# Gated attention and a mixture of experts on one core: the first group's third and fourth expert multiply their first layers in parts

## The chip, the core and the metric

The kernel runs on one core of a Trainium2 chip. A core has five engines, each with its own instruction queue that is worked off in order: PE (TensorE, matmuls; its weight loads are listed as PEld), DVE (VectorE), ACT (ScalarE), POOL (GpSimd) and SP (SyncE, which here only issues DMAs). The engines wait for each other through semaphores. The metric is device time of one launch in microseconds (us); lower is better.

## The reference

Attention with a gated state gives x, and a dense mixture of four experts follows. Everything is float32.

```python
# q, k, v, alpha: (B, H, S, D) = (4, 8, 768, 48)
for t in range(S):
    state = alpha[:, :, t, :, None] * state + np.einsum('bhd,bhe->bhde', k[:, :, t], v[:, :, t])
    y[:, :, t] = np.einsum('bhd,bhde->bhe', q[:, :, t], state)
x = y.transpose(0, 2, 1, 3).reshape(B * S, H * D)          # (3072, 384)
p = domain_probs / (domain_probs.sum(-1, keepdims=True) + 1e-09)
for e in range(4):                                         # w1: (4, 384, 1024), w2: (4, 1024, 384)
    h = np.maximum(x @ w1[e], 0.0)
    out += p[:, e:e + 1] * (h @ w2[e])
```

## The kernel before

**Units and groups.** The attention is worked in 24 units, each 128 tokens of one batch entry (`attention(u)`, a generator that yields after each step). A unit ends in 128 columns of x, written to a tile `x_raw`. The experts take the units in groups: the first group (`gi == 0`) has two units, so 256 tokens; five groups of four units (512 tokens) follow, and a last one of two. For each group the four experts run one after the other, each as a first layer (`up`, eight tiles of 128 hidden rows) and a second layer (`down`, eight steps over the hidden rows for each unit). In the first group the experts are taken in the order 1, 2, 3, 0 (`real`); "the third expert" is the one at `e == 2`, "the fourth" that at `e == 3`.

**Products in parts.** From the second group on, a first-layer tile is not one float32 product. w1 is split into a rounded top and the rest (tile `w1`, two parts; `split_piece`: an ACT copy and a DVE subtraction for each quarter of an expert), x likewise into top and low (tile `xT`; `split_x`: three ACT copies, then three DVE subtractions by `split_rest`), and a rounded copy of w1 (tile `w1s`) is loaded by a casting DMA on POOL's queue (`load_short`). Nine matmuls in the reduced format fp32r give one tile: top by top, rest by top, and `w1s` by low, for each of three row blocks. The first group instead multiplies x and w1 as they are, with three full float32 matmuls per tile (L849), while its weights are split beside it and written to DRAM tiles `kept`, from which later groups load them.

**Buffers.** `w1` and `w1s` have four buffers each, one expert. The first group's raw w1 lies in `w2r` and `w2` buffers that nobody else uses yet (`shared`); that of the fourth expert lies in `w1s` buffers (`last_w1`). The first group's x lies in the second half of its `xT` tile; later groups have `x_raw`, with one buffer.

**Order.** The order of instructions is fixed when the program is built. `advance` moves a model clock by `cost(...)` after every tile of the experts, and takes the next steps of attention units when their due times (`deal`) have come; `background` starts splits (`making`, `splitting`) and casting loads (`casts`) at the end of each tile. So an attention step stands in each engine's queue between the experts' instructions, and its place follows from the model clock, not from the chip. `cost` gives 2.6 for a tile of the first group's first layer for a full width of four units, 2.1 for one in parts.

Names that the prediction uses, with the lines of the kernel before: `one` (PSUM of a first-layer tile: L849 in full, L855 in parts), relu into `hT` (L851), `ops` (second layer, L936), accumulate into `acc` (L958), splits (L282 on ACT, L284 on DVE, L275 a POOL cast of w2), `kept` writes (L290), `w1s` loads (L232), x splits (L806 ACT, L306 DVE). Of attention: transposes `tp` (L321), scores `sc` (L607, L683, L688), `odd` and `qb` (ACT copies of q), `KT` and `QT` products (L600, L586), `lat` (score copies, ACT L698 and L701, POOL L706), result `yps` (L728), AT copy of the keys (L752), state product `sps` (L768), state update `st` (L778, L779).

Of the kernel before, what the change touches and what calls it, by code (L numbers as in the profile page):

```python
# [20 lines left out]
def kernel(  # L21
# [137 lines left out]
    last_w1 = {}  # L159
# [74 lines left out]
    def load_piece(l, i, beside=False, rest=False):  # L234
        if i >= E * NQ * LAST:
            return
        gi, k = divmod(i, E * NQ)
        e, c = divmod(k, NQ)
        if gi > l and not (l == 1 and fresh(gi, e)):
            if l == 0:  # L240
                w, short = wt[l][i] = first_parts(), first_short()
                nc.sync.dma_start(out=w.bitcast(F32), in_=kept[l][k])
                casts.append((beat[0], lambda: load_short(l, i, short)))
                return
            w = second(rest)
            nc.sync.dma_start(out=w[:, :1].bitcast(F32), in_=kept[l][k][:, 1:] if rest else kept[l][k][:, :1])
            if not rest:
                casts.append((beat[0], lambda: load_short(l, i, w[:, 1])))
            wt[l].setdefault(i, []).append(w)
            return  # L250
        if l == 1 and gi == 0 and not beside:
            return
        if l == 0:

            if e == 0:
                shared[c] = second(True)[:, 0], second(False)[:, 1]
            if e == E - 1:
                last_w1[c] = first_short()
            w = (last_w1[c] if e == E - 1 else shared[c][e % 2]).bitcast(F32)
        elif gi > 0 or e == 1:  # L260
            if c == 0:
                shared["w2"] = hid.tile([P, NQ, KC * QF], F32, name="raw2", bufs=1)
            w = shared["w2"][:, c]
        else:
            w = hidden[c][:, 0].rearrange("p f n -> p (f n)")[:, :KC * QF].bitcast(F32)
        wt[l][i] = w
        nc.sync.dma_start(out=w.rearrange("p (c n) -> p c n", c=(KC, FPQ)[l]), in_=whole_piece(l, i))

    def split_piece(l, i):
        gi, k = divmod(i, E * NQ)  # L270
        whole = wt[l][i]
        if i >= E * NQ:
            ws = wt[l][i] = [second(False), second(True)]
            top, rest = (w[:, 0] for w in ws)
            nc.gpsimd.tensor_copy(out=ws[0][:, 1], in_=whole)  # L275
        else:
            ws = [first_parts()]
            top, rest = (ws[0][:, part] for part in range(2))
            if k // NQ == E - 1:
                last_w1[k % NQ] = ws[0]  # L280
# [22 lines left out]
    def split_rest(x, out):  # L303

        top, low = out
        nc.vector.tensor_sub(low, x, top.bitcast(F32))  # L306

# [16 lines left out]
    def first_unit(fill, other):  # L324
# [160 lines left out]
        xTs[0] = work.tile([P, 2, KC, NT], F32R, name="xT", bufs=1)  # L485
        xraws[0] = xTs[0][:, 1].bitcast(F32)
# [29 lines left out]
    def attention(u):  # L516
# [197 lines left out]
        def result():  # L714
# [16 lines left out]
            if slot == 0:  # L731
                if gi == 0:
                    xTs[gi] = work.tile([P, 2, KC, NT], F32R, name="xT", bufs=1)
                    xraws[gi] = xTs[gi][:, 1].bitcast(F32)
                elif gi < LAST:
                    xraws[gi] = work.tile([P, KC * NT + PAD], F32, name="x_raw", bufs=1)[:, :KC * NT]
                    xraws[gi] = xraws[gi].rearrange("p (c n) -> p c n", n=NT)
                else:
                    xraws[gi] = []
# [71 lines left out]
    def up(gi, e, fc, slots=None):  # L811
# [16 lines left out]
        if gi == 0 and e > 0 and fc in SPLIT_AT:  # L828
            making.append(split_piece(0, e * NQ + SPLIT_AT[fc]))
        if gi == 0 and e == E - 1 and fc in (3, 6):  # L830
            making.append(split_piece(1, E * NQ + 1 + fc // 3))
# [6 lines left out]
        if gi > 0:  # L838
# [8 lines left out]
        if gi == 0:  # L847
            for kc in range(KC):
                nc.tensor.matmul(one, lhsT=w[:, kc], rhs=xraws[gi][:, kc, lo:hi],  # L849
                                 start=(kc == 0), stop=(kc == KC - 1))  # L850
            nc.scalar.activation(out=whole, in_=one, func=ACT.Relu)  # L851
        else:
            for part in (1, 2, 0):
                for kc in range(KC):
                    nc.tensor.matmul(one, lhsT=short[:, kc] if part == 1 else w[:, part // 2, kc], rhs=x_part(gi, part % 2, kc)[:, lo:hi],  # L855
                                     start=(part == 1 and kc == 0), stop=(part == 0 and kc == KC - 1))
# [7 lines left out]
        if f == FPQ - 1 and ends:  # L864
            if gi == 0:
                for k in range(2 if e == E - 2 and c > 1 else 0):
                    load_piece(0, (E - 1) * NQ + 2 * (c - 2) + k)
# [3 lines left out]
                if e == E - 1:  # L871
                    wt[0][E * NQ + c] = last_w1[c], first_short()
                    casts.append((beat[0], lambda: load_short(0, E * NQ + c, wt[0][E * NQ + c][1])))
# [13 lines left out]
    def down(gi, e, slots, between):  # L887
# [4 lines left out]
        if gi == 0 and e < E - 1 and slots[0] == (e == 0):  # L892
            making.extend(split_piece(0, first + NQ + k) for k in range(2))
        if gi == 0 and e == E - 2 and slots[0] == 1:
            making.extend(split_piece(1, E * NQ + k) for k in range(NQ // 2))
# [76 lines left out]
    def cost(layer, gi, e):  # L972
        n = len(groups[gi]) / 4
        if layer == 0:
            return 1.4 * n if fresh(gi, e) else 2.1 * n if gi > 0 else 2.6 * n
# [60 lines left out]
    with tc.manual_schedule():  # L1036
# [42 lines left out]
        for (gi, e), after in zip(tasks, [*tasks[1:], (None, None)]):  # L1079
            pieces = portions(gi, e)  # L1080
            for part in pieces:
# [6 lines left out]
                for k, slots in enumerate(turns):  # L1088
                    between = deque()
                    if following:  # L1090
# [35 lines left out]
```

## Time and profile before

| | |
|---|---|
| median of 3 runs | 965.45 us (964.46 to 966.07) |
| the profiled execution | 963.51 us; span of its instructions 961.7 us |
| PE busy | 953.7 us (99%) |
| DVE, ACT, POOL busy | 535.1, 419.2, 246.6 us |
| granted TensorE clock | 1.00 throughout |
| DMA | 246.48 MB, mean 256 GB/s |
| first group's third expert | first layer from 77.17 us, second from 91.92 us |
| first group's fourth expert | first layer from 106.27 us, second from 120.65 us |

All views come from one profiled execution. Its span is the time from the first to the last instruction; the execution's own time lies 1.8 us above it. Busy time counts what an engine executes, not what it waits for; a row of the timeline gives start, duration, engine, line, operation and, in brackets, the idle time before it and what ended it. The duration of a matmul is longer than the step to the next one, since matmuls overlap; steps are read from start to start. A full float32 matmul appears as two rows' worth of records.

### The profile page before, as it was taken

How to read it: one execution, taken by the hardware profiler on the slowest of the kernel's cores; microseconds unless marked ns; L12 is line 12 of the kernel's file. 1: busy time of each engine (PE TensorE's matmuls, PEld its weight loads, DVE VectorE, ACT ScalarE, POOL GpSimd, SP SyncE). 2: the span in 40 equal slices, each digit the busy share in tenths (PEclk: the TensorE clock that was granted, in tenths of full speed). 3: DMA queues.
4: the chain of work that ended last, by engine and by line, in shares of the span. 5: the costliest groups of instructions: out<-in, count | busy, mean ns of one | idle time of the engine just before them, and what ended most of it. 6: DMA issues, size and time to landing. Idle time of an engine off the chain costs nothing.

```text
span 961.7 us, 24843 instructions
## 1 busy us (share of the span) xinstructions
PE 953.7 (99%) x10252; PEld 851.3 (89%) x10252; DVE 535.1 (56%) x1127; ACT 419.2 (44%) x975; POOL 246.6 (26%) x403
## 2 busy tenths in 40 slices
PE   8999999999999999999999999999999999999998
PEld 7777779898998988988989889899898899999998
DVE  6766887778588555655546456646764312221312
ACT  5786766536445434344344343555435222021111
POOL 3121423344245322313312222233221202020200
PEclk9999999999999999999999999999999999999999
DMA  9889867999799999999999799989997609192921
GB/s 223 264 279 318 244 177 230 275 310 311 206 359 322 305 309 318 236 339 303 273 311 270 259 316 296 342 247 270 305 309 264 230 1 354 41 324 70 303 91 50
DMA packets 213952, 246.48 MB, mean 256 GB/s; under 512 B 95152, under 2 KB 183600, under 8 KB 213840
## 3 DMA queue, kind: packets, MB, share of 16 engines
q1 hardware_dynamic: 158800, 160.02, 56.6%
q0 software_dynamic: 54592, 84.55, 30.8%
q8 instruction: 81, 1.33, 0.6%
q10 hardware_dynamic: 448, 0.32, 0.1%
q14 instruction: 31, 0.25, 0.1%
HBM read 214.97 MB, written 29.88 MB: 255 GB/s over the span
## 4 chain that ended last, share of the span: by engine, by line
PE 94%; DVE 2%; issue 1%; ACT 1%; DMA 1%; POOL 0%; SPq 0%; DVEq 0%; ACTq 0%; POOLq 0%
PE ops L936 41%; PE one L855 38%; PE yps L728 3%; PE one L849 3%; PE sc L607 3%; PE tp L321 2%; PE sc L683 1%; DMA sk<-in_k_dram 1%; PE sps L768 1%; PE sc L688 0%; DVE QT L586 0%; DVE w2r L284 0%; ACT qb L579 0%; PE sc L380 0%; DVE KT L600 0%
## 5 line engine op out<-in xcount | busy, mean ns | idle before, releaser
L936 PE MATMUL ops<-w,hT 128*128 128x384 f32 x1408 | 254.2, 338 | 0.0
L855 PE MATMUL one<-xT,w 128*128 128x512 f32 (+1 forms) x1008 | 246.7, 380 | 0.0
L936 PEld LDWEIGHTS ops<-w,hT 128*128 128x128 f32 x1408 | 243.3, 188 | 2.5 <-issue 0.2
L857 ACT ACTIVATE hT<-one 128x512 fp32r<-128x512 f32 (+1 forms) x200 | 108.6, 547 | 279.9 <-PE one L855 278.8
L884 DVE SCALAR_TENSOR_TENSOR hT<-one,hT 128x512 fp32r<-128x512 f32 (+1 forms) x200 | 124.7, 627 | 170.3 <-ACT hT L857 170.0
L855 PEld LDWEIGHTS one<-xT,w 128*128 128x128 f32 x1008 | 184.0, 188 | 36.7
L855 PE MATMUL one<-xT,w1s 128*128 128x512 f32 (+1 forms) x504 | 141.5, 389 | 0.0
L232 POOL DMA_DIRECT2D w1s<-in_moe_w_dram x80 | 62.5, 781 | 257.5 <-PE one L855 256.9
L936 PE MATMUL ops<-w2r,hT 128*128 128x384 f32 x704 | 127.8, 337 | 0.0
L936 PEld LDWEIGHTS ops<-w2r,hT 128*128 128x128 f32 x704 | 122.1, 188 | 0.3 <-issue 0.2
L579 ACT COPY qb<-QT 64x256 f32<-64x256 f32 x230 | 92.5, 402 | 33.0 <-DVE QT L586 31.2
L855 PEld LDWEIGHTS one<-xT,w1s 128*128 128x128 f32 x504 | 89.7, 188 | 16.0 <-DVE hT L884 0.4
L586 DVE TENSOR_TENSOR QT<-QT,AT 128x256 f32<-128x256 f32 x158 | 72.6, 460 | 32.6 <-ACT qb L579 24.4
L958 DVE SCALAR_TENSOR_TENSOR acc<-ops,p_all,acc 128x384 f32<-128x384 f32 x66 | 39.6, 612 | 86.1 <-PE ops L936 85.1
L600 DVE TENSOR_TENSOR KT<-KT,AT 128x256 f32<-128x256 f32 x161 | 75.8, 471 | 0.0
L617 DVE COPY_PREDICATED near<-masks,sc 128x128 f32<-128x128 uint8 x115 | 40.9, 355 | 61.8 <-PE sc L607 59.9
L706 POOL COPY lat<-near 32x256 f32<-32x256 f32 x92 | 45.6, 496 | 96.0 <-DVE near L617 92.7
L232 POOL DMA_DIRECT2D w<-in_moe_w_dram x60 | 43.4, 727 | 96.6 <-PE ops L936 76.6
L599 ACT COPY KT<-KT 128x256 f32<-128x256 f32 x115 | 47.2, 411 | 4.6 <-PE sc L607 2.4
L570 ACT ACTIVATE odd<-QT,ident 64x256 f32<-64x256 f32 x36 | 18.8, 523 | 69.7 <-DVE QT L528 69.4
L588 DVE TENSOR_TENSOR AT<-AT 128x256 f32<-128x256 f32 (+1 forms) x138 | 42.1, 305 | 4.7
L778 POOL TENSOR_TENSOR st<-st,dec 64x192 f32<-64x192 f32 x32 | 16.7, 521 | 106.8 <-PE yps L728 105.6
(148 smaller groups left out, 997.9 us busy)
## 6 DMA issues: line engine op xcount, KB each, us to landing
w<-kept SPq DMA_DIRECT2D x76, 768.0 KB, 7.4
w1s<-in_moe_w_dram POOLq DMA_DIRECT2D x80, 384.0 KB, 8.3
w<-kept SPq DMA_DIRECT2D x60, 384.0 KB, 7.5
w<-in_moe_w_dram POOLq DMA_DIRECT2D x60, 384.0 KB, 8.9
w2r<-kept SPq DMA_DIRECT2D x60, 384.0 KB, 8.2
kept<-w POOLq DMA_DIRECT2D x16, 768.0 KB, 5.9
raw<-in_moe_w_dram SPq DMA_DIRECT2D x24, 384.0 KB, 9.7
kept<-w POOLq DMA_DIRECT2D x16, 384.0 KB, 8.5
```

The lines of the kernel that those rows point to most:

```text
L232: nc.gpsimd.dma_start(out=out.rearrange("p (c n) -> p c n", c=(KC, FPQ)[l]), in_=whole_piece(l, i))
L579: nc.scalar.copy(out=qb[rows, :, i, :].rearrange("p a (b r) -> p a b r", r=m), in_=qv[rows])
L586: nc.vector.tensor_mul(qv, qv, spread(dv[:, :, :, 0], m))
L588: nc.vector.tensor_mul(dec, dv[:, :, :, 0], dv[:, :, :, 1])
L599: nc.scalar.copy(out=new[:, :, :, 1, :], in_=old[:, :, :, 1, :])
L600: nc.vector.tensor_mul(new[:, :, :, 0, :], old[:, :, :, 0, :], spread(halved(decs[li])[:, :, :, 1], m))
L617: nc.vector.copy_predicated(near.rearrange("p a (b two r) -> p a b two r", two=2, r=m)[:, :, :, 1, :], mk.unsqueeze(1).broadcast_to([P, H, ...
L706: nc.gpsimd.tensor_copy(out=lat[rows, :, rows], in_=near[rows])
L855: nc.tensor.matmul(one, lhsT=short[:, kc] if part == 1 else w[:, part // 2, kc], rhs=x_part(gi, part % 2, kc)[:, lo:hi], start=(part == 1 ...
L857: nc.scalar.activation(out=parts[0], in_=one, func=ACT.Relu)
L884: nc.vector.scalar_tensor_tensor(out=low, in0=x, scalar=0.0, in1=top.bitcast(F32), op0=ALU.max, op1=ALU.subtract)
L936: nc.tensor.matmul(sums[slot], lhsT=h, rhs=w, start=(n == begins[slot]), stop=(n == ends[slot]))
```

## The change

The first group's third and fourth expert (`e >= PLAIN`, with `PLAIN = 2`) multiply their first layers in parts, as later groups do. For that:

- the first group's x always lies in `x_raw`, and is split beside the second expert's second layer (four steps of `split_x` at the places 0.0, 0.1, 0.2, 0.3 of its first unit);
- the third expert's w1 is split during the second expert's second layer, the fourth's during the third's second layer, all four quarters each; with every split of these experts a `w1s` load goes to POOL's queue;
- the fourth expert's raw w1 goes to the `shared` buffers, and is loaded when the second expert's second layer begins; its split parts and `w1s` serve the second group's first expert as well, which is the same expert;
- the second group's first w2 splits move from the third expert's second layer to the fourth's first layer, one at every other tile;
- `cost` counts 2.1 instead of 2.6 for the two experts' tiles, so the due times of all later attention units move.

The relu and the second layer of the first group stay as they are.

```diff
-    last_w1 = {}
+    ready = set()
+    PLAIN = 2
...
-            if e == E - 1:
-                last_w1[c] = first_short()
-            w = (last_w1[c] if e == E - 1 else shared[c][e % 2]).bitcast(F32)
+            w = shared[c][e % 2].bitcast(F32)
...
-            if k // NQ == E - 1:
-                last_w1[k % NQ] = ws[0]
+            if k >= PLAIN * NQ:
+                short = first_short()
+                load_short(0, i, short)
+                for at in [i, i + NQ] if k // NQ == E - 1 else [i]:
+                    wt[0][at] = ws[0], short
+                    ready.add(at)
...
+    def raw_x():
+        return work.tile([P, KC * NT + PAD], F32, name="x_raw", bufs=1)[:, :KC * NT].rearrange("p (c n) -> p c n", n=NT)
...
-        xTs[0] = work.tile([P, 2, KC, NT], F32R, name="xT", bufs=1)
-        xraws[0] = xTs[0][:, 1].bitcast(F32)
+        xraws[0] = raw_x()
...
-        if gi == 0 and e > 0 and fc in SPLIT_AT:
+        if gi == 0 and 0 < e < PLAIN and fc in SPLIT_AT:
             making.append(split_piece(0, e * NQ + SPLIT_AT[fc]))
-        if gi == 0 and e == E - 1 and fc in (3, 6):
-            making.append(split_piece(1, E * NQ + 1 + fc // 3))
+        if gi == 0 and e == E - 1 and fc % 2 == 0:
+            making.append(split_piece(1, E * NQ + fc // 2))
...
-        if gi > 0:
+        plain = gi == 0 and e < PLAIN
+        while gi == 0 and not plain and i not in ready:
+            background()
+        if not plain:
             w, short = wt[0][i]
...
-        if gi == 0:
+        if plain:
             for kc in range(KC):
                 nc.tensor.matmul(one, lhsT=w[:, kc], rhs=xraws[gi][:, kc, lo:hi],
                                  start=(kc == 0), stop=(kc == KC - 1))
+        else:
+            parts_of = (2, 0, 1) if gi == 0 else (1, 2, 0)
+            for part in parts_of:
+                for kc in range(KC):
+                    nc.tensor.matmul(one, lhsT=short[:, kc] if part == 1 else w[:, part // 2, kc], rhs=x_part(gi, part % 2, kc)[:, lo:hi],
+                                     start=(part == parts_of[0] and kc == 0), stop=(part == parts_of[2] and kc == KC - 1))
...
-                for k in range(2 if e == E - 2 and c > 1 else 0):
-                    load_piece(0, (E - 1) * NQ + 2 * (c - 2) + k)
...
-                if e == E - 1:
-                    wt[0][E * NQ + c] = last_w1[c], first_short()
-                    casts.append((beat[0], lambda: load_short(0, E * NQ + c, wt[0][E * NQ + c][1])))
...
-        if gi == 0 and e < E - 1 and slots[0] == (e == 0):
+        if gi == e == 0 and slots[0] == 1:
             making.extend(split_piece(0, first + NQ + k) for k in range(2))
-        if gi == 0 and e == E - 2 and slots[0] == 1:
-            making.extend(split_piece(1, E * NQ + k) for k in range(NQ // 2))
+        if gi == 0 and 0 < e < E - 1:
+            making.extend(split_piece(0, first + NQ + 2 * slots[0] + k) for k in range(2))
+        if gi == 0 and e == 1 and slots[0] == 0:
+            for k in range(NQ):
+                load_piece(0, (E - 1) * NQ + k)
...
-            return 1.4 * n if fresh(gi, e) else 2.1 * n if gi > 0 else 2.6 * n
+            return 1.4 * n if fresh(gi, e) else 2.6 * n if gi == 0 and e < PLAIN else 2.1 * n
...
+                    if gi == 0 and e == PLAIN - 1 and k == 0:
+                        between.extend((at, lambda step=step: split_x(0, step, slice(0, len(groups[0]))))
+                                       for step, at in enumerate((0.0, 0.1, 0.2, 0.3)))
```

More of the change, by code (lines that the diff above doesn't have):

```diff
@@ L731, in result @@
             if slot == 0:
-                if gi == 0:
[L733 to L739, printed above, removed]
+                xraws[gi] = raw_x() if gi < LAST else []
             if u == 1:
@@ L846, in up @@
         one = ps.tile([P, NT], F32, name="one", tag="g", bufs=4)[:, :hi - lo]
-        if gi == 0:
+        if plain:
             for kc in range(KC):
@@ L850, in up @@
                                  start=(kc == 0), stop=(kc == KC - 1))
+        else:
[4 more added lines that the diff above has]
+                                     start=(part == parts_of[0] and kc == 0), stop=(part == parts_of[2] and kc == KC - 1))
+        if gi == 0:
             nc.scalar.activation(out=whole, in_=one, func=ACT.Relu)
         else:
[L853 to L856, printed above, removed]
             nc.scalar.activation(out=parts[0], in_=one, func=ACT.Relu)
```

## The prediction

> **What bounds the kernel now.** I read the page first, then the chain of waits, then a table of busy time by stage, then the timelines of the engines in the stages that the change touches.
>
> ```profile
> PE 953.7 (99%) x10252; PEld 851.3 (89%) x10252; DVE 535.1 (56%) x1127; ACT 419.2 (44%) x975; POOL 246.6 (26%) x403
> ```
>
> PE is busy for 953.7 of 961.7 us, so in general a shorter matmul is a shorter kernel. But the chain of waits leaves PE in one place: from 100 to 138 us it runs through DVE, ACT and POOL, and from 138.61 on it is PE again. So I cut that region at the starts of its stages: first layer of the second expert (from 38.64), its second layer (63.28), then the two layers of the third (77.17, 91.92) and of the fourth (106.27, 120.65), and the second group's first tiles (132.62).
>
> ```profile
> core 0: us, PE busy (x) PEld busy (x) DVE busy (x) ACT busy (x) POOL busy (x), PEclk, DMA share, GB/s
> 38.64:63.28 24.64, 24.64 (x286) 20.64 (x284) 17.74 (x36) 19.00 (x46) 5.11 (x9) 1.00 0.97 329
> 63.28:77.17 13.89, 13.89 (x197) 8.95 (x198) 9.99 (x24) 10.26 (x26) 3.67 (x7) 1.00 0.64 191
> 77.17:91.92 14.75, 14.75 (x193) 12.79 (x192) 8.98 (x19) 10.54 (x27) 3.60 (x7) 1.00 1.06 306
> 91.92:106.27 14.35, 14.35 (x206) 9.34 (x206) 11.74 (x28) 10.12 (x23) 2.56 (x6) 1.00 0.87 286
> 106.27:120.65 14.38, 14.38 (x237) 12.45 (x236) 11.35 (x22) 12.13 (x30) 8.24 (x13) 1.00 0.90 241
> 120.65:132.62 11.97, 11.82 (x101) 7.29 (x100) 11.77 (x25) 6.83 (x19) 4.67 (x8) 1.00 0.76 206
> ```
>
> PE fills every stage, but in the last one DVE is busy for 11.77 of 11.97 us as well. Two engines are at their limit there: what PE saves before it need not come out behind it. The waits of DVE between 98 and 140 us show how much give its queue has:
>
> ```profile
> DVE w L284 <- ACT w L282: 1.4, 1, 1.4
> DVE st L779 <- POOL st L778: 1.4, 2, 1.2
> ```
>
> **The change, part by part.** First the price of a tile of the first layer (one of eight per expert), before and after:
>
> ```profile
> 77.00 2.75 PE L849 MATMUL one<-xT,w2r 128*128 128x256 f32 x12
> 79.59 0.60 PE L321 MATMUL tp<-ident,sa 128*128 128x128 f32 x4
> ...
> 141.88 0.52 PE L855 MATMUL one<-xT,w1s 128*128 128x256 f32 x3
> 142.24 0.88 PE L855 MATMUL one<-xT,w 128*128 128x256 f32 x6
> 142.96 0.52 PE L855 MATMUL one<-xT,w1s 128*128 128x256 f32 x3
> ```
>
> A full fp32 matmul is recorded twice, so the twelve rows from 77.00 to 79.59 are two tiles: 1.295 us each. Nine matmuls on parts, as the second group does them at the same width of 256, take 142.96 - 141.88 = 1.08. The change gives 0.215 per tile, 16 tiles, 3.45 us: 1.72 in each expert's stage. That is all it can win.
>
> *Splitting x.* Three ACT copies and three DVE subtractions are added in the stage from 63.28. The same split of the second group cost 1.02 us on ACT and 0.42 + 0.61 + 0.52 on DVE (128.91 to 132.3). ACT has 3.6 us free there and DVE 3.9, but ACT works in order, and in the changed program's lists the copies stand just ahead of the AT copy that PE's state product (L768) waits for. A relu that waits for the last tile now also stands ahead of the `odd` copies, 0.4 later.
>
> ```profile
> 66.56 0.58 ACT L752 COPY AT<-tp 128x512 f32<-128x512 f32 x1
> ...
> 123.53 1.02 ACT L806 ACTIVATE xT<-x_raw 128x256 fp32r<-128x256 f32 x3
> ```
>
> So the AT copy ends at 67.14 + 0.95 + 0.4 = 68.5. PE comes to the product after four second-layer matmuls (0.65 each), a transpose group (0.44) and the result (1.0), at 67.3. I take a stall of 1.15; the ends are 0 (PE late by the lost overlaps) and 1.8 (if the x_raw copy of the second group, which now waits for the last subtraction, holds the next scores too).
>
> *The third expert's weights.* The four splits (0.84 ACT, 0.95 DVE each) leave the stage at 77.17, where two ran, and all stand beside the second expert's second layer. The third DVE half follows the accumulate of the stage's last matmul, at about 80; PE needs it at the fifth tile, about 84: hidden, 0 (ends 0 and 0.5). In the stage from 77.17 the relu of the fourth tile now stands ahead of the `lat` copies on ACT; the AT copy behind them ends at about 90.0 and PE wants it at 89.65: 0.35 (0 to 0.8).
>
> *Four more loads of w1s on POOL*, 0.78 each to issue, 3.1 us; POOL is busy for 3.67 of 13.89, so issuing is hidden. The third of them stands behind a `kept` write that waits for the first split's DVE half: issued at about 74.0, wanted as the last part of the fifth tile, at 85.7. It has 11.7 us. All such loads of the run:
>
> ```profile
> DMA to landing us min/median/max: 3.4/8.3/15.5
> ```
>
> At the median it is hidden; at the worst PE waits 15.5 - 11.7 = 3.8. I take 0, since the eight w1s loads nearest in time split into four at 5.0 median (110.6 to 122.9) and four at 10.3 (156.9 to 167.0), both under 11.7. A rule of the Trainium skill speaks against it: SBUF — State Buffer, section "SBUF: two separate sides", says that a DMA issued by GpSimd can starve while VectorE holds the port pair that the two share. By that rule the added loads would be the late ones and the sum would be 3.8 worse; the four at 5.0 us landed while DVE was busy for 79% and more, so the trace does not bear it out here.
>
> *The fourth expert.* Its raw w1 loads move from 84 us to about 63 to 69, where the DMA share falls to 0.64, so this costs nothing. Its four splits move ahead of the w2 splits. After the third expert's last accumulate (107.02) DVE has six splits in the old list (two of w1, four of w2) and six in the new: its work until the second group's x is split is the same. On POOL the third `kept` write, which waits for a DVE half, now stands ahead of the `lat` copies: the copies took 2.06 us at 85.22 and 3.19 at 106.73.
>
> ```profile
> 85.22 2.06 POOL L706 COPY lat<-near 32x256 f32<-32x256 f32 x4 [2.50 <-DVE near L617]
> 106.73 3.19 POOL L706 COPY lat<-near 32x256 f32<-32x256 f32 x4
> ```
>
> They would end at 111.2 to 112.4 against PE's arrival at 110.9: a wait of 0.3 to 1.5, I take 0.6. PE then comes to the second layer 1.72 - 0.6 earlier, and meets DVE.
>
> **The sum.** Until the end of the third expert's first layer: -1.72 + 1.15 + 0.35 = -0.2. From there DVE sets the end. Its queue starts 0.2 earlier and holds the same work, so it can only gain from its waits: 1.44 + 1.42 = 2.9 us before. The wait for POOL's state product shrinks because PE gives it sooner; the wait for ACT moves from w1 to the second w2 split, and shorter ones appear. I count about 2 us left, and one `KT` product that took 1.52 beside a POOL cast at 121 instead of 0.42 should lose some of that. Gain: between 0 and 2.9, taken as 1.1. Total -0.2 - 1.1 = -1.3 us. Behind the second group's first task the lists of all five engines are the same in both programs and PE waits for nothing, so the shift stays. The profiled execution took 963.51 (span 961.7), 1.94 under the median of the runs; I expect it at 962.2, and the median at 965.45 - 1.3 = 964.1.
>
> **The rivals.**
> *The whole saving comes through.* If PE's lost overlaps hide the two ACT stalls and DVE loses its waits, -2 to -3.45 remain: 962.0 to 963.4. For it: PE itself waits for only 0.4 us in that region before, and nothing is added to DVE there. Against: DVE's 11.77 of 11.97.
> *Slower: DVE waits for ACT at each split.* From 107 on, five of six splits on DVE now directly follow their ACT half in time, and ACT is busy for 12.13 of 14.38. If each waits as the one at 112.44 did (1.44), that is 7.2 instead of 2.9, on the engine that sets the end: -0.2 + 4.3 = +4.1, 969.5. It is slower than before from 3.1 us of waits, and by over 0.2% from 5.0. Against: between splits DVE has attention work that gives ACT time; I count about 2.
> *Slower by late w1s loads,* 3.8 us in the third expert's first layer: -1.3 + 3.8 = +2.5, 967.9. It needs a landing of over 13.0 us to be slower at all; the four nearest loads speak against it. It is the case that the Trainium skill's rule named above would bring.
>
> **How the numbers follow.** 0.2% is 1.9 us, about what a measurement of this kernel can tell from no change. The forecast, a gain under 1.9 or a loss under 1.9, has 0.46; the whole saving 0.35; DVE waiting for ACT 0.13; late loads 0.06. So faster 0.35, same 0.46, slower 0.19. The forecast's own range is 963.5 to 965.5. The range takes in all of the whole saving (962.0) and the near part of the slower cases: 967.4.
>
> **What would show it.** Right: tiles of 1.08 us in the third and fourth experts' first layers; a PE wait of about 1 us at the state product near 67 to 69 us, released by the AT copy; DVE still over 95% busy in the fourth expert's second layer, with about 2 us of waits behind 107; the second group's first tile at about 131.3 instead of 132.62, and the rest of the chain shifted by as much. Wrong: that tile before 130.6 (DVE was not the bound) or after 132.62 (which wait, ACT or w1s, the chain names), or later stages that differ in length.

## The result, and the profile after

The changed kernel is slower. Its median is 974.15 us (973.46 to 975.09 in four runs) against 964.96 (964.24 to 966.07) for the kernel before on the same chip: a ratio of 1.0095, with a 95% interval of 1.0077 to 1.0112. The forecast was 964.1, in a range of 962.0 to 967.4. The profiled execution of the changed kernel took 975.09, with a span of 973.3, 11.6 more than the 961.7 before.

First the busy time of the engines, from the page of the profile after:

```profile
PE 961.0 (99%) x10300; PEld 852.6 (88%) x10300; DVE 535.6 (55%) x1130; ACT 419.8 (43%) x978; POOL 250.3 (26%) x407
```

PE is busy for 7.3 us more than before (953.7), although the change takes work from it. So other work of PE, which the change does not touch, must have become longer. The groups of instructions, with shapes kept apart, show which. Here are the 512-wide first-layer matmuls of groups 2 to 6 (912 and 456 in both programs; the columns behind the bar are the busy time and the mean ns of one). Before:

```profile
L855 PE MATMUL one<-xT,w 128*128 128x512 f32 x912 | 232.6, 391 | 0.0
L855 PE MATMUL one<-xT,w1s 128*128 128x512 f32 x456 | 132.6, 399 | 0.0
```

and after:

```profile
L856 PE MATMUL one<-xT,w 128*128 128x512 f32 x912 | 238.0, 396 | 0.0
L856 PE MATMUL one<-xT,w1s 128*128 128x512 f32 x456 | 135.1, 404 | 0.0
```

That is 373.1 against 365.2 us, 7.9 more for the same instructions in the same order. The second layer does not differ (`ops<-w,hT` is at 338 ns each in both pages). I read the start of each expert's first layer in both traces and subtracted: the second group's first tile is 3.4 us late (136.03 against 132.62), and from the second group's second expert on each expert's first layer adds about 0.4 us more, evenly, to 11.6 at the end. So the loss has three parts: 2.5 us up to the second expert's first tile, the first one 256 wide (51.46 against 48.97; the row of the prediction's table that begins at 38.64 still holds the end of the first expert), 0.9 us in the stretch from there to the second group, where the change is, and 8.2 us in the groups behind it.

The stretch of the change, as the table by stage shown for the kernel before. The rows are the second expert's two layers (here too the first row holds the end of the first expert), the third's two and the fourth's two:

```profile
core 0: us, PE busy (x) PEld busy (x) DVE busy (x) ACT busy (x) POOL busy (x), PEclk, DMA share, GB/s
41.12:65.77 24.65, 24.65 (x285) 20.64 (x284) 18.95 (x40) 18.13 (x44) 5.89 (x11) 1.00 0.90 307
65.77:81.36 15.59, 14.08 (x201) 8.91 (x201) 11.01 (x29) 13.82 (x35) 5.87 (x10) 1.00 1.24 318
81.36:95.50 14.14, 13.19 (x214) 12.45 (x213) 8.42 (x17) 9.73 (x25) 5.23 (x9) 1.00 1.08 351
95.50:109.52 14.02, 14.02 (x207) 9.13 (x205) 9.89 (x26) 9.80 (x22) 2.93 (x6) 1.00 1.08 284
109.52:124.17 14.65, 13.22 (x263) 12.36 (x261) 12.43 (x20) 11.40 (x28) 9.64 (x14) 1.00 1.12 308
124.17:136.03 11.86, 11.86 (x103) 7.19 (x101) 11.08 (x26) 6.84 (x19) 1.07 (x3) 1.00 0.22 52
```

PE's busy time falls by 1.56 us in the third expert's first layer (14.75 to 13.19) and by 1.16 in the fourth's (14.38 to 13.22): the saving is there. But PE now waits in three of the six stages, where before it waited for almost nothing. The waits of PE in this stretch of the profile after (line waited at, releaser, total, number, longest):

```profile
PE sps L766 <- ACT AT L750: 1.5, 1, 1.5
PE yps L733 <- POOL lat L711: 1.0, 1, 1.0
PE one L856 <- DMA w1s<-in_moe_w_dram: 0.9, 1, 0.9
PE sc L612 <- DVE KT L605: 0.5, 1, 0.5
```

They come to 3.9 us, more than the 2.8 us by which PE's work became shorter over the six rows.

The start-up, in the timeline of PE:

```profile
13.73 0.70 PE L386 MATMUL sc<-w,w 64*64 64x32 f32 x16 [0.26 <-ACT w1s L371]
15.86 0.38 PE L386 MATMUL sc<-w,w 64*64 64x32 f32 x13 [1.43 <-issue]
...
17.32 1.11 PE L327 MATMUL tp<-ident,hT 128*128 128x128 f32 x4
```

At 14.43 PE stops in the middle of the `sc` products for 1.43 us and waits for nothing that the profile shows ("issue"). Behind it the granted clock falls, as the table by stage shows:

```profile
16.00:17.00 1.00, 1.00 (x63) 1.00 (x59) 0.00 (x0) 0.17 (x1) 0.00 (x0) 0.96 0.09 17
17.00:18.00 1.00, 1.00 (x14) 0.94 (x10) 0.70 (x4) 0.56 (x2) 0.00 (x0) 0.50 0.87 251
18.00:19.00 1.00, 1.00 (x7) 1.00 (x6) 0.48 (x2) 0.53 (x1) 0.00 (x0) 0.50 0.96 337
```

At a clock of 0.50 four transposes take 1.11 us; before they took 0.66 at a clock of 1.00. The first group's first tile starts at 21.51 instead of 19.10. PE's list of instructions and its waits up to there are the same in both programs.

### The profile page after: what moved, and what is told of

The parts are those of the page before. It is cut to its first block, busy times and chain, and to the rows that moved or that the text cites. A ratio compares the mean times of both kernels' runs of the same rounds, so it can differ in the third digit from the quotient of the medians.

```text
span 973.3 us, 24950 instructions
## 1 busy us (share of the span) xinstructions
PE 961.0 (99%) x10300; PEld 852.6 (88%) x10300; DVE 535.6 (55%) x1130; ACT 419.8 (43%) x978; POOL 250.3 (26%) x407
## 4 chain that ended last, share of the span: by engine, by line
PE 92%; DMA 2%; ACT 2%; issue 1%; DVE 1%; POOL 1%; SPq 0%; DVEq 0%; POOLq 0%; ACTq 0%
PE ops L938 40%; PE one L856 38%; PE yps L733 3%; PE sc L612 3%; PE one L850 2%; DMA sa<-in_alpha_dram 2%; PE tp L327 1%; PE sc L688 1%; PE sps L766 1%; DMA sk<-in_k_dram 0%; ACT qb L584 0%; PE sc L693 0%; PE idle L1061 0%; POOL lat L711 0%; SPq L196 0%
## 5 line engine op out<-in xcount | busy, mean ns | idle before, releaser
L856 PE MATMUL one<-xT,w 128*128 128x512 f32 (+1 forms) x1104 | 267.2, 377 | 0.0
L856 PEld LDWEIGHTS one<-xT,w 128*128 128x128 f32 x1104 | 196.7, 188 | 42.6
L856 PE MATMUL one<-xT,w1s 128*128 128x512 f32 (+1 forms) x552 | 152.3, 384 | 0.9 <-DMA w1s<-in_moe_w_dram 0.9
L233 POOL DMA_DIRECT2D w1s<-in_moe_w_dram x84 | 65.6, 781 | 262.2 <-PE one L856 262.2
L856 PEld LDWEIGHTS one<-xT,w1s 128*128 128x128 f32 x552 | 96.6, 188 | 19.1 <-DMA w1s<-in_moe_w_dram 1.2
```

The costliest lines, as they stand in the source:

```text
L233: nc.gpsimd.dma_start(out=out.rearrange("p (c n) -> p c n", c=(KC, FPQ)[l]), in_=whole_piece(l, i))
```

## Experiments

**Where xT lies.** The change lets `x_raw` be allocated ahead of `xT`, so `xT` moves within the memory: from byte 150880 of each partition to 157184. All other tiles of the later groups keep their place, but for `x_raw`, which goes from 163168 to 150880. Four kernels move `xT`, and in each all instructions, their order and their waits are those of the kernel it starts from. The first puts `xT` back:

```
         work.tile([P, 96], F32, name="space", bufs=1)
+        xTs[0] = work.tile([P, 2, KC, NT], F32R, name="xT", bufs=1)
         xraws[0] = raw_x()
...
-        if step == 0 and lo == 0 and gi < LAST:
+        if step == 0 and lo == 0 and 0 < gi < LAST:
...
```

> The changed kernel with one edit: xT takes its place before x_raw, so that it lies where it lay in the kernel before (byte 150880 of each partition, 96 over a multiple of 128) instead of at 157184 (a multiple of 128). All instructions, their order and their waits stay. Theory A, the later groups' 8.1 us come from where xT lies: the 512-wide first-layer tiles go back from 2.107 to 2.045 us, the time falls by 8.1 to about 966.0, and the start-up stays 2.4 us long, since its instructions do not touch xT. Theory B, the later groups are slow for another reason (the stream of instructions, the clock, the DMA traffic): 974.2 as before the edit. Theory C, the start-up's 2.4 us hang on the place as well: 963.6.

The second does to the kernel before what the change did to it:

```
+        work.tile([P, KC * NT + PAD], F32, name="x_raw", bufs=1)
         xTs[0] = work.tile([P, 2, KC, NT], F32R, name="xT", bufs=1)
```

> The kernel before with one edit: x_raw takes its place ahead of xT, so that xT lies at 157184, where the changed kernel has it. Instructions, order and waits stay. Theory A (where xT lies): the 512-wide first-layer tiles of groups 2 to 6 go from 2.045 to 2.107 us and the time from 965.0 to about 973.1. The first group's first layers read xT too, but at width 256 and in full fp32; if they lengthen as well it is up to 2 us more. Theory B: 965.0. Theory C (the start-up too): first tile of the first group at 21.5 instead of 19.1 us, 975.5.

The other two separate the remainder of the address from the place, by making the tile `space` smaller by 24 or 8 elements and a later tile larger by as many:

> The changed kernel with xT ahead of x_raw and both 96 bytes lower (xT at 150784, a multiple of 128, x_raw at 163072). Theory A1, the remainder of the address counts (0 over 128 is slow, 96 is fast): 974.2, tiles at 2.107 us. Theory A2, the place counts (low is fast, high is slow, by what lies beside it or by a half of the memory): 966.0, tiles at 2.045 us. Theory B: 974.2 for this and every other place.

> The changed kernel in its own order (x_raw ahead of xT), both 32 bytes lower, so that xT lies high at 157152, which is 96 over a multiple of 128. Theory A1 (the remainder counts): 966.0, tiles at 2.045 us. Theory A2 (the place counts): 974.2, tiles at 2.107 us. Theory B: 974.2.

Measured, beside 964.58 for the kernel before on the same chip: 965.76 with `xT` back (ratio 1.0015, interval 1.0005 to 1.0026); 973.08 for the kernel before with `xT` moved (1.0088, 1.0072 to 1.0105); 974.82 low at a multiple of 128 (1.0105, 1.0090 to 1.0120); 971.71 high at 96 over 128 (1.0075, 1.0058 to 1.0092). The groups of the four in this order, `one<-xT,w` alone:

```profile
L857 PE MATMUL one<-xT,w 128*128 128x512 f32 x912 | 232.6, 390 | 0.0
```

```profile
L856 PE MATMUL one<-xT,w 128*128 128x512 f32 x912 | 238.1, 396 | 0.0
```

```profile
L857 PE MATMUL one<-xT,w 128*128 128x512 f32 x912 | 238.1, 396 | 0.0
```

```profile
L857 PE MATMUL one<-xT,w 128*128 128x512 f32 x912 | 236.8, 395 | 0.0
```

Theory A holds both ways: 8.4 us go with the address in the changed kernel (974.15 to 965.76; 8.0 if each is compared with the kernel before as measured beside it) and 8.5 come with it in the kernel before. Theory C does not hold: the first group's first tile starts at 20.73 with `xT` back, and at 19.26 in the kernel before with `xT` moved. Neither of the finer theories holds: the low place can be slow, so the place does not decide, but 96 over 128 isn't quick everywhere (971.71, neither 966 nor 974). The remainder over 128 is not the rule.

**With what xT must agree.** To find the rule, `xT` was put into a larger tile and started at another byte in each group, so that one run gives five addresses:

```
+    PLACES = [96, 96, 88, 80, 72, 64]
...
+    def at_place(gi):
+        size = 2 * KC * NT
+        tile_of = work.tile([P, 96 + size], F32R, name="xT", bufs=1)[:, PLACES[gi]:PLACES[gi] + size]
+        return tile_of.rearrange("p (t c n) -> p t c n", t=2, n=NT)
...
-        work.tile([P, 96], F32, name="space", bufs=1)
+        xTs[0] = at_place(0)
...
-            xTs[gi] = work.tile([P, 2, KC, NT], F32R, name="xT", bufs=1)
+            xTs[gi] = at_place(gi)
```

> A measurement of the address by itself: the changed kernel, instructions, order and waits as they are, but xT lies in a larger tile, at another start in each group of chunks. Starts over a multiple of 2048 bytes: group 2 at 1376, group 3 at 1344, group 4 at 1312, group 5 at 1280, group 6 at 1248. Read is the interval between the starts of successive 512-wide first-layer matmuls, group by group (known so far: 227 ns at 1376, 234 at 1280 and 1536, 232 at 1504). Theory R1, the remainder over 128 bytes decides: 227 in group 2, 234 in group 5, 227 again in group 6 (1248 is 96 over a multiple of 128). Theory R2, the distance from where the weights lie (864 over 2048) decides over a longer period: group 6 is not back at 227, and the intervals move steadily from group to group. Theory B, something else in the program: the same interval in all groups.

> As the run with one start per group before it, with starts over 2048 of 1360, 1328, 1216, 1152 and 1088 bytes for groups 2 to 6. Theory R1 (the remainder over 128): 1152 gives 234 ns, 1216 and 1088 (both 64 over 128) agree with each other, and 1360 and 1328 (80 and 48 over 128) lie between their neighbours. Theory R2 (a longer period): 1216 and 1088 differ.

> A third run with one start of xT per group, over 2048: 1120, 1888, 1632, 864 and 1372 bytes for groups 2 to 6 (the weights of the first layer lie at 864 and 1888, all 352 over a multiple of 512; so far only 1376, which is also 352 over a multiple of 512, gave 227 ns, and eleven other starts 232 to 236). Theory R3, xT is quick only where it lies 352 over 512: 227 in groups 3 (1888) and 5 (864), 232 or more in groups 2, 4 and 6. Theory R4, it is quick at 96 over 256: 227 in groups 2 to 5. Theory R5, only 1376 over 2048 is quick: 232 or more in all five. At 1372, one element off, 230 or more under each.

In the next two the weights were moved as well, by one small tile ahead of all of them (`wts.tile([P, 32], F32, name="shift", bufs=1)`), and then by a second one behind `w1`, so that `w1s` and all that follows keep their remainder over 256:

> As the third run with one start per group, but all weight tiles lie 128 bytes higher (the first layer's at 480 over 512 instead of 352), and xT starts at 1376, 1504, 1888, 2016 and 1120 over 2048. Theory W, what counts is that xT and the weights that are loaded beside its matmuls start alike over 512 bytes: 227 ns in group 3 (1504) and group 5 (2016), 232 or more in groups 2, 4 and 6. Theory X, the start of xT alone counts: 227 in group 2 (1376) and wherever the third run with one start per group was quick, and 232 in group 3 (1504).

> One start of xT per group once more, with one of the two weight tiles of the first layer moved: w1 (6 of a tile's 9 matmuls) lies 224 over 256 bytes, w1s (3 of 9) and everything else stay at the remainder over 256 that they have. Starts of xT over 256 in groups 2 to 6: 96, 224, 112, 96, 128. Theory W, the stationary tile that a matmul runs with or loads beside it is what xT has to agree with: with xT at 96 the intervals behind w1s matmuls are 227 ns and those behind w1 matmuls 232, with xT at 224 the other way round. Theory V, it is not the weights but the tiles that moved along with them in the run before (KT, QT, AT, w2): 227 in groups 2 and 5 for all nine, 232 in group 3.

> A last run with one start of xT per group: 16, 48, 64, 80 and 112 bytes above the remainder of the weights over 256 (1392, 1424, 1440, 1456 and 1488 over 2048). So far equal remainders gave 227 ns and every other distance 230 to 236; the second layer's 384-wide matmuls, whose moving weights lie 64 bytes above the stationary tile, run at 173 ns, 13 over 384 columns at 2.4 per ns, which is as little as 227 is over 512 columns. Theory 1, only equal remainders are quick: 230 or more in all five groups. Theory 2, a distance of 64 is as quick or quicker, as in the second layer: 227 or less in group 4.

The mean interval between the starts of successive 512-wide matmuls of one expert (those under 300 ns, that is without the pauses between tiles), worked out from the records of the traces, by the distance of `xT` from the weights over 256 bytes:

```
distance (bytes)   start of xT over 2048, weights at 864        ns
   0               1376, 1120, 1888, 1632, 864                  227.2 to 229.0
   0               1504, 2016 (weights moved to 992)            227.6 to 228.8
  -4               1372                                         230.0
 +16               1392                                         231.5
 +32               1152                                         233.1
 +48               1424                                         232.8
 +64               1440                                         229.3
 +80               1456                                         231.0
 +96               1216                                         233.3
+112               1488                                         231.0
+128               1248, 1504                                   232.4
+128               1376, 1888, 1120 (weights moved to 992)      232.1 to 233.4
 -16               1360                                         236.1
 -32               1344, 1088                                   233.1
 -48               1328                                         233.8
 -64               1312                                         233.3
 -96               1280, 1536                                   234.2
```

Theory B, R1 and R5 fall with the first three of these runs, R3 with 1120 and 1632, which are quick without being 352 over 512; R4 (96 over 256) fits until the weights move. R2 is right in that the distance from the weights counts, but not in a longer period: 1216 and 1088 don't differ. Then 1376 becomes slow and 1504 quick: theory W, but with 256 bytes as the period and not 512, since 1120 and 1632 were quick. The run in which `w1` alone moved shows it within one tile. With `xT` at 96 over 256 (group 2) the median interval between two `w1s` matmuls is 228 ns and between two `w1` matmuls 232; with `xT` at 224 (group 3) it is 233 and 227. So theory V falls. The remaining run found no distance that beats an equal remainder: theory 2 there falls. Theory 1 had put every other distance at 230 or more, and 64 came out just under it, at 229.3 (median 229, against 227 for equal remainders).

So a 512-wide matmul here starts soonest behind the other when the moving tile and the stationary weights have equal remainders over 256 bytes: a mean of 227.2 to 229.0 ns and a median of 227, against means of 229.3 to 236.1 and medians of 229 to 235 at the fourteen other distances tried. Why, and which of the two reads waits, is not shown by these runs.

**The waits in the stretch of the change.** Two kernels, both with `xT` back at 150880. The first divides the first group's x earlier:

```
                     up(gi, e, fc, part)
+                    if gi == 0 and e == PLAIN - 1 and fc >= 4:
+                        split_x(0, fc - 4, slice(0, len(groups[0])))
...
-                    if gi == 0 and e == PLAIN - 1 and k == 0:
-                        between.extend((at, lambda step=step: split_x(0, step, slice(0, len(groups[0]))))
-                                       for step, at in enumerate((0.0, 0.1, 0.2, 0.3)))
```

> The changed kernel with xT back at 150880 and the first group's division of x moved from the start of the second expert's second layer to the last four tiles of its first layer, where ACT and DVE have idle time (ACT idle 2.64 us before 65.15). Theory 1, the wait of 1.5 us at the sps tiles is bought by ACT's three x copies (1.03 us) and DVE's subtractions ahead of the copy AT: the wait falls to 0.5 or less and the time from 965.8 to about 964.6. Theory 2, the wait is that of the older queue on ACT (the odd, lat and qb copies): it stays at 1.0 or more, time 965.5 to 965.8.

The second loads the third expert's `w1s` sooner:

```
...
         if gi == 0 and e == 1 and slots[0] == 0:
             for k in range(NQ):
                 load_piece(0, (E - 1) * NQ + k)
+                soon[2 * NQ + k] = first_short()
+                load_short(0, 2 * NQ + k, soon[2 * NQ + k])
```

> The changed kernel with xT back at 150880 and the third expert's four w1s loads issued together when the second expert's second layer begins, not one with each split. Theory 1, the late load (12.0 us from issue to landing, PE waits 0.95 to 1.4 for it) costs just its wait: 965.8 falls to about 964.5. Theory 2, the DVE chain of the fourth expert's stage (99% busy there in the kernel before) takes back what is gained ahead of it: the wait disappears, the waits for lat (0.9) and KT (0.5) grow, and the time is 965.3 to 965.8.

The waits of PE in the stretch, with the early division of x and then with the early loads:

```profile
PE one L857 <- DMA w1s<-in_moe_w_dram: 1.1, 1, 1.1
PE yps L734 <- POOL lat L712: 0.9, 1, 0.9
PE sps L767 <- ACT AT L751: 0.5, 1, 0.5
PE sc L613 <- DVE KT L606: 0.4, 1, 0.4
```

```profile
PE sps L770 <- ACT AT L754: 1.9, 2, 1.5
PE yps L737 <- POOL lat L715: 0.9, 1, 0.9
PE sc L616 <- DVE KT L609: 0.5, 1, 0.5
```

In the first the wait for the AT copy falls from 1.5 to 0.5, in the second the wait for the load is gone, and a wait of 0.4 shows at another state product (1.9 in two). The waits for `lat` and `KT` did not grow. The stretch from the second expert's first tile to the second group's takes 84.02 and 84.04 us, against 85.19 with `xT` back and neither edit; 83.65 before the change. But 85.19 is the longest of eleven profiles of the changed list of instructions with neither edit: they go from 84.01 to 85.19, and with them the wait for the load. Where it is 0.3 us or less the stretch takes 84.01 to 84.07, at 0.8 to 1.2 us 84.51 to 84.85, at 1.4 us 85.04 and 85.19. So the early loads give what the load was late in that execution, 0 to 1.2 us: theory 1 there, of varying size. The early division gives about 0.8 of the 1.0 us by which its wait fell (84.02 with a wait for the load of 1.1, against 84.79 at 1.1 without the edit); there is one profile with the edit. The medians do not tell: 965.32 (ratio 1.0002, 0.9989 to 1.0014) and 965.82 (1.0013, 0.9999 to 1.0026), beside 964.60.

Both edits in one kernel:

> xT at 150880, the division of x in the last four tiles of the second expert's first layer, and the third expert's w1s loads issued together: both edits of the two runs before in one kernel. Theory 1, the two gains add (each was 1.15 to 1.17 us between the second expert's first tile and the second group's first): that stretch takes 82.9 us, 0.75 less than in the kernel before (83.65), and the median, 965.8 with neither edit, falls to 963.5 or 964. Theory 2, the DVE chain of the fourth expert's stage takes one of them back: 84.0, median 965.

The stretch takes 83.23 us, 0.4 less than before the change and 0.3 more than expected: in this profile the two gains add, and two waits of 0.8 us together stay at state products, one of them hidden before by the late load. A later run with the same two edits (the last one of the start-up below) took 83.68, as much as before the change, so the 0.4 is not sure. And the median is 966.12 beside 965.25 (1.0004, 0.9991 to 1.0017): no difference from the kernel before. This profile's span is 3.2 us longer than that of the kernel before (964.9 against 961.7). The start-up takes 2.25 of it, and 1.15 more are lost in the second group, from the start of its second expert to that of its third: 40.79 us, against 39.64 to 39.66 in three profiles with the list of before and `xT` in its place. PE stands still there at `yps` for 0.76 us without a releaser. It does so in eight of the nineteen profiles, for 0.15 to 0.76 us; with `xT` back and no other edit:

```profile
PE yps L734 <- issue: 0.5, 1, 0.5
```

**The start-up.** The trace records DMA packets of 16 KB of instructions. In the profile before the first of them lands at 12.52, in the profile after at 14.54, with PE's wait behind it. That they are PE's is read from the order: in every profile with such a wait without a releaser, at `sc` or at `y`, PE goes on 1.0 to 1.5 us after one has landed, and in the second group too (with `xT` back a packet lands at 204.26 and PE goes on at 205.62). Second profiles of both programs, and one of the kernel before made as long as the changed one:

> The changed kernel as it is, a second profile. Theory 1, the start-up's 2.4 us belong to the execution (the landing of TensorE's first packet of instructions, 12.5 us in the kernel before and 13.2 to 14.5 in the runs with the changed kernel's instructions, beside saturated DMA engines): the first tile of the first group begins anywhere from 19.4 to 21.5, with the wait at another length. Theory 2, it belongs to the program: 21.5 again, with a wait of 1.4 us and a granted clock of 0.5 from 17 to 20 us.

> The kernel before as it is, a further profile. Theory 1, the start-up's length belongs to the execution (when TensorE's first packet of instructions lands): the first tile of the first group begins anywhere from 19.1 to 21.5 us here too. Theory 2, it belongs to the program: 19.1 to 19.3, as in the two profiles of this list of instructions so far.

> The kernel before with 96 idle matmuls of 128 columns behind the last expert, so that TensorE's list is as long as in the changed kernel (7258 matmuls against 7162), and everything up to there as before. Only the start is read. Theory 1, execution: 19.1 to 21.5. Theory 2a, the longer list is what moves the landing of the first packets: wait at the sc matmuls of 0.5 us or more, first tile after 20.0. Theory 2b, it is something else in the changed program: 19.1 to 19.3.

```
                     down(gi, e, slots, between)
+        idle = ps.tile([P, DM], F32, name="idle", tag="g", bufs=4)
+        fill(96)
```

The changed kernel's second profile has its first tile at 20.89, the packet at 13.78, waits of 0.7 and 1.4. The kernel before starts it at 19.30 and, with the longer list, at 19.48. Taking all profiles together, the list of before gives 19.10 to 19.48 (four profiles, packet at 12.5 to 13.3), and the changed list 19.39 to 21.51 (fourteen, packet at 12.9 to 14.5, about 20.3 in the middle). In six of the fourteen the granted clock is 0.50 for 3.4 us in the start-up, in none of the four. So the start-up varies from one execution to the next, by 2 us with the changed list; but it is also later with it, and the length of the list is not why (2a falls). What in the changed program makes it so is open.

Last, whether the packet is late by the data that are loaded beside it: two weight pieces issued later.

```
-        for i in range(NQ // 2):
-            load_piece(0, i)
         load(2, "k")
...
         load(2, "q")
-        for i in range(NQ // 2, NQ):
+        for i in range(NQ):
             load_piece(0, i)
```

> The kernel with both edits (division of x and w1s loads early, xT at 150880), and the first two weight pieces of the first expert issued 4 us later, together with the other two, so that 0.79 MB less are asked for while TensorE's first packet of instructions is on its way. Theory 1, the packet is late because the DMA engines are full of data: it lands at 12.5 or before, the waits of 0.5 to 1.5 us at the sc matmuls go, the first tile begins near 19.2 and the median falls from 966.1 to about 964. Theory 2, the packet is late for another reason: the wait stays, or the weights themselves come late (a wait of PE for the DMA of w2r at the first tile), and the median stays at 966 or rises.

```profile
20.88 0.56 PE L504 MATMUL y<-w1s,rv 128*32 128x64 f32 x12 [2.76 <-issue]
21.74 2.50 PE L852 MATMUL one<-x_raw,w2r 128*128 128x128 f32 x10 [0.30 <-ACT x_raw L507]
```

The first packet lands at 12.90 and the wait at `sc` is gone, but the second now lands at 19.61, where the loads were put, and PE waits 2.76 us for it at `y`. The median is 968.36 beside 965.75 (1.0026, 1.0011 to 1.0041): slower. Neither theory came as it was put: the wait at `sc` went, but the packet was not at 12.5 and the gain did not come. The first half tells little, since the changed list had its first packet at 12.88 in another profile, without this edit. The second half fits packets that queue with the data, as 19.61 is later than in any other profile (16.9 to 19.0); it is one profile, and that they queue is not shown beyond it. None of the kernels tried beats the kernel before.

## Why the prediction was wrong, step by step

- **"Behind the second group's first task the lists of all five engines are the same in both programs and PE waits for nothing, so the shift stays."** This is the step that failed. The lists are the same, and PE waits for nothing; but the same matmuls read `xT` from another address and take longer: 8.2 us in the profile, 8.0 to 8.4 in the medians. Without it the changed kernel stands at 965.76, inside the range, but 1.2 us above the kernel before where 1.3 below was forecast: it would be inside for the wrong reason, since start-up and waits took more than the saving. And that PE waits for nothing there did not hold in every execution: with `xT` back it stops in the second group behind a packet of instructions, which costs 0.9 us (40.52 instead of 39.64). The diff shows the moved allocation; I read it as a change of order only. One sign that was named in advance as proof of error, later stages that differ in length, is what happened; the other, the second group's first tile after 132.62, came as well (136.03).
- **The price of a tile.** Right. In the timeline of the profile after a tile of the fourth expert is 111.59 - 110.53 = 1.06 us (1.08 forecast):

```profile
110.53 0.52 PE L856 MATMUL one<-xT,w1s 128*128 128x256 f32 x3
110.88 0.88 PE L856 MATMUL one<-xT,w 128*128 128x256 f32 x6
111.59 0.52 PE L856 MATMUL one<-xT,w1s 128*128 128x256 f32 x3
```

- **Splitting x.** The mechanism was right, and the place; the size was 1.51 us instead of 1.15, within the ends of 0 and 1.8. (The sum put the three copies at 0.95, where the row shown beside it has 1.02.) The three ACT copies stand from 69.82 to 70.87, right ahead of the AT copy:

```profile
69.82 1.03 ACT L804 ACTIVATE xT<-x_raw 128x256 fp32r<-128x256 f32 x3
70.87 0.58 ACT L750 COPY AT<-tp 128x512 f32<-128x512 f32 x1
```

  Moving them took 1.0 us of the wait away, about the 1.03 us that they take; the other 0.5 is the older queue on ACT.
- **The third expert's weights.** The stall of 0.35 taken for the relu ahead of the `lat` copies does not show in the profile after, where PE comes to that stage's state product (93.87) late, after its wait for the load. In the kernel with both edits, where the load is early, it is there and of the right size: 0.37 at 92.23, released by the AT copy.
- **Four more loads of w1s,** taken at 0. Wrong by 0.95 us in the profile after, and by 0 to 1.4 in the ten others of its list of instructions with neither edit. The load that was late was the fourth, issued at 80.34 behind a `kept` write, and it took 12.0 us to land; in those others it took 11.3 to 12.6, always the longest of the eight. The prediction had worked out a time for the third only (11.7 us to spare, 8.8 taken), and had held the eight nearest loads, at 5.0 and 10.3 median, against it. The 0.95 is a quarter of the rival "late w1s loads" (3.8 us). That rival was also the case of the Trainium skill's page SBUF — State Buffer, section "SBUF: two separate sides", by which a DMA issued by GpSimd can starve while VectorE holds the shared port pair. Issued sooner, none was late (at most 8.2 us to land). The runs don't tell whether VectorE held it, or the `kept` writes ahead of it on the same queue, or the DMA engines, whose share in that stage rose from 0.64 to 1.24, with the fourth expert's w1 loads that were taken to cost nothing there.
- **The fourth expert.** The wait for POOL's `lat` copies was 0.95 instead of 0.6, within 0.3 to 1.5.
- **DVE sets the end.** Half right. In the fourth expert's second layer DVE was busy for 11.08 of 11.86 us, 93% and not over 95%, and that stage shortened by 0.11 only (11.97 to 11.86). But PE was busy for all 11.86 of it, and the gain of 1.1 that was to come from DVE's waits did not: the fourth expert's first layer became longer by 0.27 (14.38 to 14.65), since its 1.16 less of PE work was met by 1.43 of waits for `lat` and `KT`. With both edits the stretch took 83.23 us in one profile, less by both gains, so DVE did not take them back there; in another it took 83.68.
- **The start-up** was not in the sum at all; the reason is the same, that equal lists were taken to be equal time. It cost 2.5 us in the profiled execution, and less in the other profiles of that list (first tile at 19.39 to 21.35, against 19.10 to 19.48 with the list of before). The Trainium skill's page TensorE: Matmul & The Clock Gate, section "Why this matters for your kernels", asks for no gaps of PE over some 3 us if the clock is to stay up; here the granted clock fell to 0.50 behind a wait of 1.43 us, among small matmuls, so on that the trace differs.
- **The rivals.** Neither "the whole saving" nor "DVE waits for ACT" came: DVE's longest wait for ACT at a split was 1.3 us, and there was one of it.

## What to carry to other kernels

When a diff moves an allocation, compare the addresses of the tiles in both programs before saying that stages with equal instruction lists take equal time: 6 ns per matmul times 1368 matmuls is 8.2 us, more than all that the change was about. Where PE streams one tile against another without a break, try equal remainders of the two addresses over 256 bytes, and read the intervals between starts, not the mean of one.

Here PE was busy for 99% with hardly a wait, and what was saved on it was spent on waits that the change uncovered. In such a kernel, look at the nearest releasers (here ACT's copies, a load, POOL's copies) together with the saving, and compare one profile with several of the same list of instructions before calling a difference of 1 us a gain.

## What was not expected of the hardware

- The moving and the stationary operand of 512-wide matmuls interact by their addresses: a median of 227 ns from start to start with equal remainders over 256 bytes, 229 to 235 at fourteen other distances, and reversed by moving the weights.
- Packets of TensorE's instructions can come late enough to stop it: the first landed anywhere from 12.5 to 14.5 us, and when loads were put off into the second packet's time that one landed at 19.61 instead of 16.9 to 19.0, with a wait of 2.76 us.
- The granted clock in the start-up does not follow from the length of one wait: it was 0.50 for 3.4 us behind waits of 1.43, 1.22 (x divided early) and 0.69 us (`xT` high at 96 over 128), and stayed at 1.00 behind one of 1.15 (`xT` back).
